# Row sums of a finished chunk, one score run later in a two-layer attention and spectral kernel

## The chip, the cores and the metric

The kernel runs on one core of a Trainium2 chip. The time is that of one execution on the device, in microseconds (us): the median of several runs. One further execution was recorded by the hardware profiler; its rows are what the texts below quote. The engines are PE (TensorE: matmuls, with PEld for its weight loads), DVE (VectorE), ACT (ScalarE), POOL (GpSimd) and SP (SyncE, which here issues DMAs). Each engine runs its own instructions in order; semaphores make one wait for another.

## What is computed

The reference is two layers, each a multi-head attention with a residual, and a filter in the frequency domain with a residual. The attention is what matters here:

```python
def _A_ref(x, wqkv, wo):
    B, S, D = x.shape            # 1, 2048, 1024
    H = 32                       # heads of 32
    Dh = D // H
    qkv = (x @ wqkv).reshape(B, S, 3, H, Dh).transpose(2, 0, 3, 1, 4)
    q, k, v = qkv[0], qkv[1], qkv[2]
    scores = jnp.einsum("bhqd,bhkd->bhqk", q, k) * (Dh ** -0.5)
    p = _softmax(scores, axis=-1)
    o = jnp.einsum("bhqk,bhkd->bhqd", p, v)
    return o.transpose(0, 2, 1, 3).reshape(B, S, D) @ wo
...
x = A_x
x = x + _A_ref(_layernorm(x), A_wqkv, A_wo)
x = x + _B_ref(_layernorm(x), B_w_r, B_w_i)      # rfft2, times W, irfft2
x = x + _A_ref(_layernorm(x), A_wqkv, A_wo)
x = x + _B_ref(_layernorm(x), B_w_r, B_w_i)
```

## The kernel before

The 32 heads are worked on in 8 groups of 4 (`g`, 0 to 7). Within a group the 2048 queries are cut into 4 chunks of 512 (`c`), and the 2048 keys into 16 tiles of 128 (`kt`). One (`c`, `kt`) is a unit; a group has 64 units, a layer 512. For a unit three things are done:

- `S` (line 548 in the profile, called a score run below): 12 matmuls give the scores of four heads in two PSUM tiles `s` (each 128 x 1024, two banks); ACT turns each into exponentials `p` (L552). The scores are transposed: keys stand on the partitions, queries along the free axis. The pool of `s` has three tiles, that of `p` eight.
- `PV` (L558): the value matmuls of the unit, four heads side by side in 32 columns each, add into one PSUM bank `o`, which holds the chunk's output until the 16th unit; then ACT copies it out (L562).
- `add` (L571): DVE adds the two tiles `p` of the unit to two accumulators `acc[0]` and `acc[1]` in SBUF, which in the profile stand under the tile name `R`. Unit 0 of a chunk adds nothing; unit 1 starts the accumulators anew from the tiles of units 0 and 1 (L569), so it overwrites what the chunk before left there. There is one pair of accumulators.

When a chunk is finished, `fin` (lines 573 to 585) makes the divisors of the softmax. Four matmuls of `acc` with a matrix of ones (L577) sum over the partitions into one `s` tile (named `z`); eight records in the profile. DVE transposes `z` (L578), takes the reciprocal (L580), keeps a running maximum (L581), spreads it (L583) and multiplies the copied output by it (L584). Later `out` (L590, L591, L593) writes the product out: a cast on ACT, a difference on POOL, a DMA on SP.

Between these steps a generator, called the filler, puts other work on PE: in every odd unit some 8 to 24 matmuls of the projections for coming groups, Q and K (`qk_chunk`, L328) or V (`v_tiles`, L372). A projection's chunk adds up in one PSUM bank `x` (the pool has one buffer); for Q and K, ACT casts it to its high half (L167) and DVE computes the low half (L168), and only after that may PE write the next projection into `x`. A projection also takes weights that are split in the same way (L168 with `wst`; in the first layer followed by a maximum, L257). When Q or K of a group is whole, four small matmuls (L345) and a reduction on DVE (L347) give its norms, by which the exponentials are shifted. Even groups carry Q and K projections (12 chunks of 24 steps), odd groups one Q and then V. Group 6 loads the output projection's weights beside its units, and group 7 carries that projection's first part (L431, L451).

The order of PE and ACT in this stage is the order in which the code is written (`manual_schedule`); the order of DVE, POOL and SP is chosen by the framework's scheduler when the program is built. The written order around a chunk's end is set by the loop over `u` (printed below). `pend` holds units whose value matmuls are still to come: at each even `kt` the two units before are done in one run of eight matmuls. `late` holds the same units for `add`, one at each unit. So, with units 14 and 15 of chunk c left over:

- unit 0 of the next chunk: scores, then the value matmuls of units 14 and 15, `add` of 14
- unit 1: scores, `add` of 15, and `fin` of the finished chunk; then filler
- unit 2: scores, the value matmuls of units 0 and 1
- unit 3: scores, `add` of 1 (L569), filler
- unit 5: `out`

`fin` is called in the loop 31 times per layer, 62 in all; the last chunk of each layer has its own call behind the loop.

Of the kernel before, what the change touches and what calls it, by code (L numbers as in the profile page):

```python
# [266 lines left out]
def attention(nc, tc, layer, ap, xin, yd, wts, wo, cst, dram, flags):  # L267
# [116 lines left out]
    def sums(ph):  # L384
        return 8 if ph[0] == "v" else 4

    def filler():
        run(prep(phases[0]))
        for i, ph in enumerate(phases):
            nxt = prep(phases[i + 1]) if i + 1 < len(phases) else iter(())  # L390
            for n in range(sums(ph)):
                yield from (v_tiles if ph[0] == "v" else qk_chunk)(ph, n)
                for _ in range(1 + (n > 0)):
                    next(nxt, None)
            run(nxt)
# [6 lines left out]
    def load_wo():  # L402
        st = []

        def load(i):
            if i < 16:
                s = sgp.tile([128, 512], F32, name="wst")
                nc.sync.dma_start(s, wo[i // 2 * 128:i // 2 * 128 + 128, i % 2 * 512:i % 2 * 512 + 512])
                st.append(s)
        load(0)  # L410
        load(1)
        for i in range(16):
            load(i + 2)
            d, sl = i // 2, slice(i % 2 * 512, i % 2 * 512 + 512)
            split(nc, wo_t[0][d // 4][:, d % 4, sl], wo_t[1][d // 4][:, d % 4, sl], st[i], SW)
            yield
# [51 lines left out]
    def wo_parts():  # L468
        load_o(0)
        load_o(1)  # L470
        for t in [2, 3, 0, 1] + list(range(4, 12)):
            if t == 8:
                two = wvp.tile([128, 2, 1024], F32, name="wv")
                wo_dst[8], wo_dst[9] = two[:, 0], two[:, 1]
            yield from wo_part(t // 4, t % 4, wo_dst[t])
            if t in (1, 7):
                load_o(t // 4 + 2)
# [64 lines left out]
    def S(g, c, kt):  # L542

        s = [psS.tile([128, 2, 512], F32, name="s") for _ in range(2)]
        for i, (a, b) in enumerate(((0, 0), (0, 1), (1, 0))):
            for h in range(4):
                r = slice(32 * h, 32 * h + 32)
                nc.tensor.matmul(s[h // 2][:, h % 2], K[g][r, a, kt * 128:kt * 128 + 128],  # L548
                                 Q[g][r, b, c * 512:c * 512 + 512], start=i == 0, stop=i == 2)
        for hf in range(2):  # L550
            p = P[g, c, kt, hf] = pp.tile([128, 2, 512], F32, name="p")
            nc.scalar.activation(p, s[hf], AF.Exp, bias=bias[g], scale=SCALE / (SQ * SQ))  # L552
# [12 lines left out]
    def add(g, c, kt):  # L565
        for hf in range(2):
            p = P[g, c, kt, hf]
            if kt == 1:
                nc.vector.scalar_tensor_tensor(acc[hf], P[g, c, 0, hf], 1e-34, p, op0=ALU.add, op1=ALU.add)  # L569
            elif kt:  # L570
                nc.vector.tensor_add(acc[hf], acc[hf], p)  # L571

    def fin(g, c):
        zt = on.tile([128, 16, 32], F32, name="zt")
        z = psS.tile([128, 2, 512], F32, name="s")[:, 0]
        for h in range(4):
            nc.tensor.matmul(z[32 * h:32 * h + 32], cst["ones"], acc[h // 2][:, h % 2], start=True, stop=True)  # L577
        nc.vector.transpose(zt.rearrange("p a b -> p (a b)"), z)  # L578
        rc = sm.tile([128, 16], F32, name="rc")
        nc.vector.reciprocal(rc, zt[:, :, 0])  # L580
        nc.vector.tensor_max(flags["r"], flags["r"], rc)  # L581
        r = on.tile([128, 512], F32, name="zt")
        nc.vector.transpose(r.rearrange("p (a b) -> p a b", b=32), rc.unsqueeze(2).broadcast_to([128, 16, 32]))  # L583
        nc.vector.scalar_tensor_tensor(r, O[g, c], SO, r, op0=ALU.mult, op1=ALU.mult)  # L584
        O[g, c] = r
# [8 lines left out]
        else:  # L594
            olast[c] = t

    pend, done, late = [], [], []
    fill, lwo, wof = filler(), load_wo(), wo_parts()
    left, parts, rests = 16, 20, list(range(12))

    def slots(f, sums, n, steps):

        while sums:
            k = max(1, int(n / sums + 0.5))
            m = -(-steps // k)
            for i in range(0, steps, m):
                while left_norms:
                    norms()
                for _ in range(min(m, steps - i)):
                    next(f, None)  # L610
                n -= 1
                yield sums - (i + m >= steps)
            sums -= 1

    with tc.manual_schedule(engines={mybir.EngineType.PE, mybir.EngineType.Activation}):
        for g in range(NG):
            todo = sum(sums(ph) for ph in beside.get(g, []))
            sl = slots(fill, todo, 22 if g == NG - 2 else 32, 24)
            wsl = slots(wof, 4, 10, 21)
            for u in range(NCH * NKT):  # L620
                c, kt = divmod(u, NKT)
                S(g, c, kt)
                if kt % 2 == 0:
                    for w in pend:
                        PV(*w)
                    late = pend
                    pend = []
                for w in late[:1]:
                    add(*w)
                    if w[2] == NKT - 1:  # L630
                        fin(*w[:2])
                        done = [w[:2]]
                late = late[1:]
                if kt == 5 and done:
                    out(*done.pop())
                pend.append((g, c, kt))
                if kt % 2 == 0:
                    continue
                if todo:
                    todo = next(sl)  # L640
                elif g == NG - 2:
                    if left:
                        run(lwo)
                        left = 0
                    if next(wsl, None) is not None and u == NCH * NKT - 1:
                        run(wsl)
                elif g == NG - 1:
                    t = rests[0] if rests else 16
                    if (t // 4 < c - 1 or t // 4 == c - 1 and kt >= 7) and (kt % 4 == 3 or not parts):
                        wo_rest(rests.pop(0))  # L650
                    elif parts:
                        parts -= 1
                        for _ in range(21):
                            next(wof)
                if g == NG - 2 and todo < 4:
                    for _ in range(2):
                        if left > (8 if todo == 3 else 0):
                            next(lwo, None)
                            left -= 1
        for w in pend:  # L660
            PV(*w)
        for w in late + pend:
            add(*w)
        run(wof)
        for t in rests:
            wo_rest(t)
# [537 lines left out]
```

## Time and profile before

| what | value |
|---|---|
| median of 3 runs | 3942.41 us (3938.75 to 3947.32) |
| profiled execution | 3932.85 us |
| its span, first to last instruction | 3931.1 us |
| mean granted TensorE clock | 0.987 |
| score stage, first layer | about 130 to 1670 us of the span |
| score stage, second layer | about 2100 to 3620 us of the span |
| largest group of DVE | L571, 1792 adds, 2145.1 us busy |
| largest group of ACT | L552, 2048 exponentials, 2170.0 us busy |
| largest groups of PE | L558 984.9 us, L328 688.8 us, L548 432.3 and 432.0 us busy |

How to read the rows. In a timeline a row has the start in us from the span's start, the busy time in us, the engine, line and operation, then the written tile, an arrow and the tiles read, the shape and the number of instructions that were merged into the row; in square brackets stands the idle time of the engine before it and what ended that. In a table of groups the numbers behind the bar are the busy time in us, the mean of one in ns, and the idle time before the group's instructions with what ended it. "R", "Q", "x", "s", "o", "p" are tile names of the program. A busy PE is not PE at its peak: matmuls overlap, and the ends are modelled; the starts are recorded. Rows are merged, so that a short wait inside a run shows as a longer row and not as idleness.

### The profile page before, as it was taken

What the parts mean: (1) busy time and instruction counts of PE and PEld (TensorE: products, weight loads), DVE (VectorE), ACT (ScalarE), POOL (GpSimd) and SP (SyncE); (2) the same over time, 40 slices, a digit from 0 to 9 for tenths busy, and PEclk for the clock granted to TensorE, in tenths of its full rate; (3) what the DMA queues carried; (4) which work ended last, traced back from release to release, by engine and by line L of the source; (5) the groups of instructions that cost most, each with busy time, mean ns of one, the idle gap of its engine ahead of it and who ended that gap; (6) DMA issues with size and microseconds to landing.
All of it is one profiled execution on the core that took longest, in us unless ns stands there. A gap on an engine that the chain in (4) does not pass through costs nothing.

```text
span 3931.1 us, 80082 instructions
## 1 busy us (share of the span) xinstructions
PE 3764.3 (96%) x33204; PEld 1667.9 (42%) x33204; DVE 3188.9 (81%) x3865; ACT 2896.0 (74%) x3561; POOL 644.0 (16%) x589
## 2 busy tenths in 40 slices
PE   7999999999999999989989999999999999999798
PEld 5322432342233233368863334333432432333688
DVE  6689898989898877866666998899898888788454
ACT  4587887788788765558746888888888787665586
POOL 1111011101110200004321220122021212000143
PEclk9999999999999999999999999999999999999999
DMA  3000000000000211143120000000000002111333
GB/s 116 15 12 22 12 12 17 17 12 20 12 23 9 90 49 68 60 159 125 59 87 12 20 18 12 12 17 23 9 18 17 17 12 89 56 70 56 135 110 105
DMA packets 97560, 177.32 MB, mean 45 GB/s; under 512 B 7200, under 2 KB 52896, under 8 KB 96160
## 3 DMA queue, kind: packets, MB, share of 16 engines
q1 hardware_dynamic: 97040, 172.03, 12.7%
q8 instruction: 262, 4.29, 0.4%
q14 instruction: 114, 0.93, 0.1%
q10 hardware_dynamic: 144, 0.07, 0.0%
HBM read 123.83 MB, written 48.23 MB: 44 GB/s over the span
## 4 chain that ended last, share of the span: by engine, by line


## 5 line engine op out<-in xcount | busy, mean ns | idle before, releaser
L552 ACT ACTIVATE p<-s,bias 128x1024 f32<-128x1024 f32 x2048 | 2170.0, 1112 | 586.2 <-PE s L548 575.1
L571 DVE TENSOR_TENSOR R<-R,p 128x1024 f32<-128x1024 f32 x1792 | 2145.1, 1249 | 145.5 <-ACT p L552 141.3
L558 PE MATMUL o<-p,R 128*32 128x512 f32 x8192 | 984.9, 598 | 0.0
L328 PE MATMUL x<-big,wqk 128*128 128x512 f16 x2880 | 688.8, 385 | 22.9 <-DVE R L168 8.2
L548 PEld LDWEIGHTS <-R 32*128 32x128 f16 x12288 | 231.1, 92 | 782.6 <-issue 666.3
L328 PEld LDWEIGHTS <-wqk 128*128 128x128 f16 x3072 | 278.0, 98 | 463.8 <-issue 173.5
L548 PE MATMUL s<-R 32*128 32x512 f16 x6144 | 432.3, 379 | 19.9 <-ACT p L552 16.4
L548 PE MATMUL s<-Q,R 32*128 32x512 f16 x6144 | 432.0, 378 | 11.9 <-ACT p L552 10.6
L558 PEld LDWEIGHTS o<-p,R 128*32 128x32 f32 x8192 | 213.7, 109 | 523.5 <-issue 523.0
L591 POOL TENSOR_TENSOR ohl<-zt,ohl 128x512 f16<-128x512 f32 x62 | 180.1, 2905 | 1471.9 <-ACT ohl L590 1471.9
L372 PEld LDWEIGHTS <-big 128*128 128x128 f16 x3072 | 292.2, 98 | 116.5 <-issue 69.6
L372 PE MATMUL x<-wv,big 128*128 128x256 f16 x2688 | 321.2, 276 | 12.4 <-DVE R L168 5.8
L569 DVE SCALAR_TENSOR_TENSOR R<-p 128x1024 f32<-128x1024 f32 x128 | 153.8, 1203 | 199.0 <-ACT p L552 198.7
L332 POOL TENSOR_TENSOR sq<-R 128x512 bf16<-128x512 f16 x96 | 142.3, 1482 | 700.3 <-ACT R L167 699.8
L431 PE MATMUL x<-big 128*128 128x512 f16 x1008 | 228.0, 380 | 0.0
L431 PEld LDWEIGHTS <-big 128*128 128x128 f16 x1344 | 126.7, 98 | 177.7 <-issue 35.5
L881 DVE TENSOR_TENSOR H<-G,H 128x512 f16<-128x512 f32 (+1 forms) x68 | 46.7, 687 | 104.5 <-ACT H L880 104.4
L833 PE MATMUL ps<-cbi,H 128*128 128x256 f16 (+1 forms) x792 | 99.1, 273 | 5.6 <-ACT H L880 3.7
L826 ACT COPY U<-ps 64x256 f32<-64x256 f32 (+1 forms) x272 | 97.2, 357 | 8.4 <-PE ps L833 3.3
L826 ACT COPY B<-ps 64x256 f32<-64x256 f32 (+1 forms) x272 | 97.1, 357 | 6.7 <-PE ps L833 2.4
L332 POOL TENSOR_TENSOR sq<-Q 128x512 bf16<-128x512 f16 x32 | 45.1, 1409 | 324.3 <-ACT Q L167 324.3
L833 PE MATMUL ps<-cb,big 128*128 128x256 f16 x780 | 96.3, 273 | 0.0
(419 smaller groups left out, 3100.8 us busy)
## 6 DMA issues: line engine op xcount, KB each, us to landing
wst<-in_wp SPq DMA_DIRECT2D x96, 256.0 KB, 3.0
R<-y SPq DMA_DIRECT2D x32, 512.0 KB, 5.2
w<-in_w SPq DMA_DIRECT2D x60, 256.0 KB, 2.6
od<-ohl SPq DMA_DIRECT2D x56, 256.0 KB, 2.4
big<-od SPq DMA_DIRECT2D x16, 896.0 KB, 7.1
y<-R SPq DMA_DIRECT2D x20, 512.0 KB, 2.6
R<-in_x SPq DMA_DIRECT2D x16, 512.0 KB, 6.7
wst<-in_wo SPq DMA_DIRECT2D x32, 256.0 KB, 2.9
```

What stands on the lines that cost most here:

```text
L328: nc.tensor.matmul(ps, a, b, start=d == 0 and i == 0, stop=d == 7 and i == 2)
L332: nc.gpsimd.tensor_tensor(nrm[ph][:, c], t[:, 0], t[:, 0], op=ALU.mult)
L372: nc.tensor.matmul(ps[:, j], l, r, start=d == 0 and i == 0, stop=d == 7 and i == 2)
L431: nc.tensor.matmul(p, a, b, start=start and d == ds[0] and i == 0, stop=stop and d == ds[-1] and i == 2)
L548: nc.tensor.matmul(s[h // 2][:, h % 2], K[g][r, a, kt * 128:kt * 128 + 128], Q[g][r, b, c * 512:c * 512 + 512], start=i == 0, stop=i == 2)
L552: nc.scalar.activation(p, s[hf], AF.Exp, bias=bias[g], scale=SCALE / (SQ * SQ))
L558: nc.tensor.matmul(O[g, c][32 * h:32 * h + 32], V[g][:, kt, 32 * h:32 * h + 32], P[g, c, kt, h // 2][:, h % 2], start=kt == 0, stop=kt == ...
L569: nc.vector.scalar_tensor_tensor(acc[hf], P[g, c, 0, hf], 1e-34, p, op0=ALU.add, op1=ALU.add)
L571: nc.vector.tensor_add(acc[hf], acc[hf], p)
L591: eng.tensor_tensor(t[:, 1], r, t[:, 0], op=ALU.subtract)
L826: nc.scalar.copy(ov[64 * r:64 * r + 64, a0:a0 + m, x], tl[64 * x:64 * x + 64, :m, r])
L833: nc.tensor.matmul(out, l, r, start=k == 0, stop=k == len(mm_) - 1)
```

## The change

`fin` of the finished chunk is no longer called in unit 1, behind the `add` of unit 15, but in unit 2, behind that unit's scores and ahead of the value matmuls of units 0 and 1. That is the third score run of the new chunk. In unit 1 the chunk is only noted in `ends`. What `fin` does, the number of instructions and the call for the last chunk of a layer, behind the loop, stay as they were.

```diff
-    pend, done, late = [], [], []
+    pend, ends, done, late = [], [], [], []
...
                 S(g, c, kt)
                 if kt % 2 == 0:
+                    if ends and kt == 2:
+                        fin(*ends[0])
+                        done = [ends.pop()]
                     for w in pend:
                         PV(*w)
                     late = pend
...
                 for w in late[:1]:
                     add(*w)
                     if w[2] == NKT - 1:
-                        fin(*w[:2])
-                        done = [w[:2]]
+                        ends = [w[:2]]
                 late = late[1:]
                 if kt == 5 and done:
                     out(*done.pop())
```

## The prediction

> **What bounds the kernel now.** I read the page's busy shares first, then the windows over the score stages, then the groups of PE and DVE, and last the timeline of single engines around the ends of chunks. The page, and one window over most of the first layer's score stage (columns: length, then busy of PE, weight loads, DVE, ACT, POOL, clock, DMA):
>
> ```profile
> PE 3764.3 (96%) x33204; PEld 1667.9 (42%) x33204; DVE 3188.9 (81%) x3865; ACT 2896.0 (74%) x3561; POOL 644.0 (16%) x589
> 170.00:1280.00 1110.00, 1087.91 (x10280) 384.35 (x10276) 1000.50 (x1013) 897.16 (x954) 133.44 (x96) 1.00 0.05 16
> ```
>
> PE sets the pace, 98% busy in this window; but DVE is at 90%, so 2.4 us of new DVE idleness in a chunk of some 45 us takes half of its reserve. The groups (busy, mean ns | idle before, releaser):
>
> ```profile
> L577 PE MATMUL s<-R,ones 128*32 128x512 f32 x512 | 73.1, 604 | 1.4 <-DVE R L571 1.4
> L571 DVE TENSOR_TENSOR R<-R,p 128x1024 f32<-128x1024 f32 x1792 | 2145.1, 1249 | 145.5 <-ACT p L552 141.3
> L569 DVE SCALAR_TENSOR_TENSOR R<-p 128x1024 f32<-128x1024 f32 x128 | 153.8, 1203 | 199.0 <-ACT p L552 198.7 <-PE s L577 0.3
> ```
>
> L577 are the row sums (64 times 8 records). L569 is the first add of the next chunk: it overwrites the accumulator that L577 reads, so it may not run before it; today its 199 us of idleness are ended by exponentials. PE at two chunk ends, then DVE at the first:
>
> ```profile
> 177.28 2.08 PE L577 MATMUL s<-R,ones 128*32 128x512 f32 x8
> 179.29 1.90 PE L328 MATMUL x<-big,wqk 128*128 128x512 f16 x8
> 181.13 0.82 PE L548 MATMUL s<-R 32*128 32x512 f16 x12
> 181.88 1.92 PE L558 MATMUL o<-p,R 128*32 128x512 f32 x16
> ...
> 222.52 1.06 PE L577 MATMUL s<-R,ones 128*32 128x512 f32 x8
> 223.52 2.76 PE L328 MATMUL x<-big,wqk 128*128 128x512 f16 x12
> ```
> ```profile
> 175.90 2.35 DVE L571 TENSOR_TENSOR R<-R,p 128x1024 f32<-128x1024 f32 x2
> 178.54 1.23 DVE L569 SCALAR_TENSOR_TENSOR R<-p 128x1024 f32<-128x1024 f32 x1 [0.28 <-ACT p L552]
> ```
>
> At 177.28 the last adds end at 178.25 and PE loses 1 us (2.08 against 1.06). That is the exception: 73.1 less 64 x 1.065 leaves 4.9 us for all row sums.
>
> **The change, part by part.** On PE, first chunk end of the first layer (s is a score or row-sum tile, o the value product, x the filler's), before and then now:
>
> ```order
> L548 MATMUL s<-R 128x512
> L577 MATMUL s<-R,ones 32x512 x4
> L328 LDWEIGHTS wqk
> L328 MATMUL x<-big,wqk 128x512
> ```
> ```order
> L548 MATMUL s<-R 128x512
> L577 MATMUL s<-R,ones 32x512 x4
> L558 MATMUL o<-p,R 32x512 x8
> L548 LDWEIGHTS R
> ```
>
> The row sums move behind a filler run and a score run. DVE at the same place, before and now:
>
> ```order
> L569 SCALAR_TENSOR_TENSOR R<-p 128x1024
> L578 STREAM_TRANSPOSE zt<-s 128x512
> L569 SCALAR_TENSOR_TENSOR R<-p 128x1024
> L580 RECIPROCAL rc<-zt 128x16
> L168 SCALAR_TENSOR_TENSOR R<-x,R 128x512
> L581 TENSOR_TENSOR fr<-fr,rc 128x16
> L583 STREAM_TRANSPOSE zt<-rc 128x512
> L584 SCALAR_TENSOR_TENSOR zt<-oc,zt 128x512
> L571 TENSOR_TENSOR R<-R,p 128x1024 x12
> ```
> ```order
> L168 SCALAR_TENSOR_TENSOR R<-x,R 128x512
> L569 SCALAR_TENSOR_TENSOR R<-p 128x1024
> L578 STREAM_TRANSPOSE zt<-s 128x512
> L569 SCALAR_TENSOR_TENSOR R<-p 128x1024
> L580 RECIPROCAL rc<-zt 128x16
> L571 TENSOR_TENSOR R<-R,p 128x1024
> L581 TENSOR_TENSOR fr<-fr,rc 128x16
> L583 STREAM_TRANSPOSE zt<-rc 128x512
> L571 TENSOR_TENSOR R<-R,p 128x1024
> L584 SCALAR_TENSOR_TENSOR zt<-oc,zt 128x512
> L571 TENSOR_TENSOR R<-R,p 128x1024 x10
> ```
>
> The filler's split L168 goes ahead where it falls there, two adds slip between the small steps; nothing else jumps the queue. ACT, POOL and SP keep their order, so no DMA moves in its queue.
>
> *What stays covered.* The row sums need a score tile, the one that the second exponential of the score run before frees:
>
> ```profile
> 177.39 2.12 ACT L552 ACTIVATE p<-s,bias 128x1024 f32<-128x1024 f32 x2
> ```
>
> It ends at 179.51, which is 2.23 after the old place of the row sums at 177.28, and the new place comes 2.59 after it: no new wait, by 0.36. ACT's cast L590 needs L584's result; it stands behind the exponentials of the fourth score run after the moved row sums, some 10.9 us after they start (value, score, filler, score, value, score run, exponentials), and L584 is done about 8 us after. Were that cover gone, ACT would stand still in order, and PE with it.
>
> *Gains.* The 4.9 us go: the adds end at most 1 us after the old place, and the new one is 2.6 us later. Beside them, the row sums stand directly ahead of the value matmuls. 8 records take 1.00 (222.52 to 223.52; each run's busy time overlaps the next by 0.06) and 16 take 1.92 - 0.06 = 1.86, so a run costs 2 x 1.00 - 1.86 = 0.14 that doesn't depend on its length, and two runs made one save up to 0.14 at each of 62 places, 8.9 us. If a joined run keeps its 0.14, the sum below is 3.5 higher. The Trainium skill (TensorEngine Tiling (Array Packing), Tiling Modes) says that changing the tiling mode drains the array and changing only the tile doesn't; both runs are 128*32, so by it the whole 0.14 goes; no row of before has such a pair.
>
> *The cost.* L569 waits for the moved row sums, and all DVE work queues behind it. A chunk end of the second layer, PE and then DVE:
>
> ```profile
> 2143.44 1.07 PE L577 MATMUL s<-R,ones 128*32 128x512 f32 x8
> ...
> 2166.01 1.89 PE L328 MATMUL x<-big,wqk 128*128 128x512 f16 x8 [0.36 <-DVE R L168]
> ```
> ```profile
> 2144.69 1.23 DVE L569 SCALAR_TENSOR_TENSOR R<-p 128x1024 f32<-128x1024 f32 x1 [2.12 <-ACT p L552]
> 2145.83 0.71 DVE L578 STREAM_TRANSPOSE zt<-s 128x512 f32<-128x512 f32 x1
> 2146.47 1.18 DVE L569 SCALAR_TENSOR_TENSOR R<-p 128x1024 f32<-128x1024 f32 x1
> 2147.57 0.24 DVE L580 RECIPROCAL rc<-zt 128x16 f32<-128x16 f32 x1
> ...
> 2148.51 0.70 DVE L583 STREAM_TRANSPOSE zt<-rc 128x512 f32<-128x512 f32 x1
> 2149.24 0.69 DVE L584 SCALAR_TENSOR_TENSOR zt<-oc,zt 128x512 f32<-128x512 f32 x1
> 2149.84 15.51 DVE L571 TENSOR_TENSOR R<-R,p 128x1024 f32<-128x1024 f32 x12
> 2165.28 0.68 DVE L168 SCALAR_TENSOR_TENSOR R<-x,R 128x512 f16<-128x512 f32 x1
> ```
> ```profile
> 2161.30 4.06 DVE L571 TENSOR_TENSOR R<-R,p 128x1024 f32<-128x1024 f32 x2
> ```
>
> From the start f of the old row sums: the new ones start at f + 1.84 (filler, 179.29 to 181.13) + 0.75 (scores, to 181.88) = f + 2.59; they end 1.07 later, so L569 starts near f + 3.7 instead of f + 1.25. By start-to-start times, L569 1.14, L578 0.64, L569 1.10, L580 and L581 0.4, L583 0.73, L584 0.60 and two adds at 1.14 make 6.9: DVE stands at f + 10.6 where it stood, after its two adds, at 2149.84 + 2.28 - 2143.44 = f + 8.7. It is 1.9 late. Twelve adds run in one piece (the excess over 1.14 each is mostly slow adds, the row at 2161.30, which is two adds at 2.0, and not waiting), then comes the split L168 that frees the only PSUM bank x, for which PE already waits. So 1.8 reaches PE. Elsewhere the slack between L168's end and PE's next filler is subtracted:
>
> ```profile
> 228.82 2.35 DVE L571 TENSOR_TENSOR R<-R,p 128x1024 f32<-128x1024 f32 x2
> 237.74 1.34 DVE L257 TENSOR_REDUCE wm<-wst 128x1 f32<-128x512 f32 x2 [0.82 <-DMA wst<-in_wp]
> 246.92 0.68 DVE L168 SCALAR_TENSOR_TENSOR Q<-x,Q 128x512 f16<-128x512 f32 x1
> ```
> ```profile
> 247.65 2.53 PE L328 MATMUL x<-big,wqk 128*128 128x512 f16 x11 [2.38 <-DVE Q L168]
> ```
> ```profile
> 502.16 1.06 PE L577 MATMUL s<-R,ones 128*32 128x512 f32 x8
> 518.77 0.60 PE L328 MATMUL x<-big,wqk 128*128 128x512 f16 x2
> ```
> ```profile
> 508.01 9.22 DVE L571 TENSOR_TENSOR R<-R,p 128x1024 f32<-128x1024 f32 x8
> 517.15 0.69 DVE L168 SCALAR_TENSOR_TENSOR R<-x,R 128x512 f16<-128x512 f32 x1
> ```
> ```profile
> 387.12 3.51 PE L372 MATMUL x<-wv,big 128*128 128x256 f16 x16 [2.06 <-DVE R L168]
> ```
> ```profile
> 2293.66 2.36 DVE L571 TENSOR_TENSOR R<-R,p 128x1024 f32<-128x1024 f32 x2 [0.17 <-ACT p L552]
> 2295.94 0.68 DVE L168 SCALAR_TENSOR_TENSOR R<-x,R 128x512 f16<-128x512 f32 x1
> ```
> ```profile
> 2281.61 0.40 PE L345 MATMUL s<-sq,bones 128*32 128x512 bf16 x4 [0.21 <-ACT p L552]
> ...
> 2297.56 1.68 PE L328 MATMUL x<-big,wqk 128*128 128x512 f16 x7
> ```
>
> By kind of chunk end (even and odd g, from chunk to chunk), both layers:
> - even, 0 to 1, 8 places: 1.8; in three of the first layer some 0.5 less, since the old stall goes: 13.
> - even, 1 to 2, 6 places: the filler run at 223.52 is 2.70 long, so the row sums start at f + 3.46, DVE stands at f + 11.5 instead of 228.82 + 2.28 - 222.52 = f + 8.6, 2.9 late. In the first layer the wait for a weight load (0.82 at 237.74) is filled by an add that the new order puts behind the weight splits; the slack at 247.65 is nil, since PE waited there already: 2.0. The second layer has no such wait and no stall: 2.9 less a slack that I take, as below, at 0.9: 12 in all.
> - odd 3 to even 0, 6 places: first add at f + 5.85, so 10.6 - 5.85 - 2.28 = 2.5 late; slack 518.77 - 517.84 = 0.93: 1.5 each: 9.
> - even 3 to odd 0, 6 places: the same slack, 2297.56 - 2296.62 = 0.94 (the last rows), 0.17 of DVE's waiting that takes up lateness, and the 0.2 that the norm matmuls (L345) wait there for a score tile behind the row sums goes: 1.2: 7.
> - odd 0 to 1: PE waits for L168 at 387.12 in the first layer, 3 places. The chunk begins 1.2 late by the kind before, so that only part of a new 1.8 is added: between 0 and 1.8, taken at 1.3: 4. In the second layer no PE wait on L168 stands there, and I count none.
> - even 2 to 3 (6) and g = 6, 1 to 2 (2): between 0 and 1.9, taken at 0.9: 7.
> - the other 25, with V products or output projection beside them: no split that PE waits for, -0.14 each: -3.5.
>
> The sum is +48 us. The profiled execution took 3932.85 (span 3931.1), so 3981 by it; the runs' median is 3942.41, 9.6 higher, so 3990. The measurement can tell some 0.2% (8 us) from no change.
>
> **Rivals.** *The lateness is swallowed.* Then only gains are left: 4.9, 1.3 (six times the 0.21 at 2281.61) and 8.9: -15, 3927. For it: DVE has 110 us idle in that window. Against it: no idleness stands between the row sums and L168 at 2165.28 or 517.15. It decides from the point at which DVE idles 1.9 ahead of that split. 0.07.
>
> *Only places where PE already waits pay.* The eight, three and three places above with a wait in their rows give 13 + 6 + 4 = 23, less the 15: +8, 3950, within 0.2%. It needs the slack elsewhere to be 1.5 more than the rows show. 0.07.
>
> *The longer waits cost clock too.* One wait of 2.1 us was followed by twelve slow filler matmuls:
>
> ```profile
> 614.45 4.07 PE L328 MATMUL x<-big,wqk 128*128 128x512 f16 x12 [2.08 <-DVE Q L168]
> ```
>
> against 2.76 at 223.52, 1.3 more; at 247.65 no such loss followed 2.38. Six waits of the first layer, the three like 247.65 and the three like 387.12, grow to about 4: 6 x 1.3 to 2.6 is 8 to 16, so 3998 to 4006. The Trainium skill (TensorE: Matmul & The Clock Gate, Part 1) puts half clock behind an idle window of about 3.4 us, which speaks for this case. 0.2.
>
> *The change doesn't do what it says*: the order of PE above rules it out.
>
> **How the numbers follow.** The main case has 0.66, with 3972 to 4000 as its own range: lower if L569 may start half a microsecond earlier (some 32 places, -16), higher with the unknown kinds at 1.9. The range 3957 to 4008 adds the clock case and part of the rest. Slower: 0.66 + 0.2 = 0.86; same 0.07; faster 0.07.
>
> **What would show it.** Right: L569's idleness grows from 199 to about 330 us and its releaser becomes L577; L577 falls to some 66 busy; the idleness of PE ahead of its filler (below for L328), which L168 ends, grows by some 45 in all; row sums and value matmuls together take 2.72, not 2.86.
>
> ```profile
> L328 PE MATMUL x<-big,wqk 128*128 128x512 f16 x2880 | 688.8, 385 | 22.9 <-DVE R L168 8.2 <-DVE Q L168 6.5 <-ACT wqk L167 5.4
> ```
>
> Wrong: L328's idleness stays near 23 us, or L569 still starts 1.25 after the score run ahead of the row sums' old place.

## The result, and the profile after

| | before | after |
|---|---|---|
| median of 4 runs | 3940.58 us (3935.93 to 3947.32) | 4050.73 us (4044.13 to 4057.25) |
| profiled execution's span | 3931.1 us | 4052.0 us |
| mean granted clock | 0.987 | 0.975 |
| ratio after / before | | 1.0282, 95% interval 1.027 to 1.0295 |

The change costs 110 us. The forecast said slower, by the mechanism that came, but by 48 us; 4050.7 lies outside its range of 3957 to 4008.

The page of after, and then the groups that the prediction named (busy, mean ns of one | idle before, releaser):

```profile
PE 3796.4 (94%) x33204; PEld 1688.2 (42%) x33204; DVE 3203.0 (79%) x3865; ACT 2893.7 (71%) x3561; POOL 577.9 (14%) x589
```
```profile
L571 DVE TENSOR_TENSOR R<-R,p 128x1024 f32<-128x1024 f32 x1792 | 2182.5, 1268 | 116.9 <-ACT p L552 115.1
L328 PE MATMUL x<-big,wqk 128*128 128x512 f16 x2880 | 716.2, 396 | 107.8 <-DVE R L168 70.6 <-DVE Q L168 28.8 <-ACT wqk L167 5.4
L569 DVE SCALAR_TENSOR_TENSOR R<-p 128x1024 f32<-128x1024 f32 x128 | 155.6, 1217 | 183.3 <-PE s L577 139.7 <-ACT p L552 43.5
L577 PE MATMUL s<-R,ones 128*32 128x512 f32 x512 | 68.2, 605 | 0.0
```

The row sums (L577) lost their stalls, 73.1 to 68.2. L569's main releaser is now L577, 139.7 us. And L328's idle time went from 22.9 to 107.8 us, where 45 more were forecast. Its busy time went from 688.8 to 716.2 as well: the same 2880 records of filler matmuls take 27 us longer. The span's 121 us are 32 more of PE's busy time (3764.3 to 3796.4) and 89 of its idle time.

The waits of PE on the low-half split, the view of waits of before and then of after (us in total, times, longest):

```profile
PE x L328 <- DVE R L168: 8.2, 8, 2.4
...
PE x L328 <- DVE Q L168: 6.5, 3, 2.4
PE x L372 <- DVE R L168: 5.8, 3, 2.1
```
```profile
PE x L328 <- DVE R L168: 70.6, 29, 3.1
PE x L328 <- DVE Q L168: 28.8, 8, 5.0
...
PE x L372 <- DVE R L168: 23.9, 6, 4.7
```

20.5 us became 123.3, in 43 waits in place of 14. So the chain of the prediction is there: row sums later, L569 later, DVE late, split late, PE waits for its bank.

One place shows why the waits are twice as long as forecast. It is the end from an odd group to an even one whose rows of before stand in the prediction (502.16 to 518.77). PE of after, from the moved row sums on:

```profile
521.66 1.06 PE L577 MATMUL s<-R,ones 128*32 128x512 f32 x8
522.54 1.90 PE L558 MATMUL o<-p,R 128*32 128x512 f32 x16
...
534.78 0.83 PE L548 MATMUL s<-R 32*128 32x512 f16 x12
538.71 2.72 PE L328 MATMUL x<-big,wqk 128*128 128x512 f16 x6 [3.10 <-DVE R L168]
```

DVE of after at the same place, then POOL of after, and POOL of before at its place:

```profile
522.81 1.23 DVE L569 SCALAR_TENSOR_TENSOR R<-p 128x1024 f32<-128x1024 f32 x1 [6.23 <-PE s L577]
...
529.34 8.71 DVE L571 TENSOR_TENSOR R<-R,p 128x1024 f32<-128x1024 f32 x6
535.99 2.06 DVE L571 TENSOR_TENSOR R<-R,p 128x1024 f32<-128x1024 f32 x1
537.97 0.68 DVE L168 SCALAR_TENSOR_TENSOR R<-x,R 128x512 f16<-128x512 f32 x1
```
```profile
533.14 1.85 POOL L591 TENSOR_TENSOR ohl<-zt,ohl 128x512 f16<-128x512 f32 x1 [43.14 <-ACT ohl L590]
534.95 2.02 POOL L332 TENSOR_TENSOR sq<-R 128x512 bf16<-128x512 f16 x1
```
```profile
516.43 1.82 POOL L591 TENSOR_TENSOR ohl<-zt,ohl 128x512 f16<-128x512 f32 x1 [43.54 <-ACT ohl L590]
518.22 2.02 POOL L332 TENSOR_TENSOR sq<-R 128x512 bf16<-128x512 f16 x1
```

The six adds from 529.34 to L168 take 537.97 - 529.34 = 8.63 us; at 1.14 each they would take 6.84. The row at 535.99, from a narrower window, shows the last of these six alone; it takes 2.06: it is the one that meets POOL's square L332, and the one ahead of it meets the difference L591. In before, L591 began at 516.43 and L168 at 517.15: no add stood between the two, and those that POOL slowed came behind the split. DVE's lateness has carried the way to the split into POOL's work. The add at 535.99 ends at 538.05, 1.08 after L332's end at 536.97, which is about an add's usual 1.14: it stood still until POOL was done. The Trainium skill (SBUF — State Buffer, "SBUF: two separate sides") says that a VectorE step with two inputs in SBUF, as an add is, and a GpSimd step share one pair of ports as an exclusive lock, held for a whole instruction, and that the other side blocks; this trace agrees, with the 1.08 us.

Counted over the 40 chunk ends with a split of the filler behind them, in one trace of each kernel: of the adds between L569 and the first such split, 80 took over 1.5 us in after (two at every end) and 19 in before, and all these adds together took 52.5 us longer. The split began 3.05 us later in the mean, measured from the chunk's first score run; 1.3 of that are the slow adds, the other 1.7 are the lateness that L569's wait leaves.

What follows the wait, in windows of after (columns as in the prediction's first window: length, PE, weight loads, DVE, ACT, POOL, clock, DMA):

```profile
534.43:537.84 3.41, 1.18 (x16) 0.32 (x13) 3.41 (x2) 3.26 (x4) 2.54 (x2) 1.00 0.23 77
537.84:541.26 3.42, 2.55 (x7) 0.88 (x7) 3.42 (x5) 0.00 (x0) 0.00 (x0) 0.50 0.02 5
541.26:544.67 3.41, 3.41 (x23) 0.80 (x25) 1.93 (x2) 0.96 (x1) 0.00 (x0) 0.50 0.00 0
```

The granted clock is 0.50 from 537.84, still within the wait, to 544.67. The row at 538.71 shows six of the filler run's eight matmuls, as its view ends there: they take 2.72, where all eight took 1.90 at 179.29 in before.

The starts of the score runs in the two traces give the loss of each chunk (start of its first score run to that of the next chunk's, after minus before). By the prediction's kinds, with two controls that are told below beside it (all in us, each from one profiled execution of each kernel):

| chunk end | places | forecast | measured | run e2 (late DVE, no move on PE) | POOL's steps mostly left out (e13 less e14) |
|---|---|---|---|---|---|
| even, 0 to 1 | 8 | 13 | 17.4 | 17.7 | 6.3 |
| even, 1 to 2 | 6 | 12 | 26.4 | 17.3 | 15.2 |
| odd 3 to even 0 | 6 | 9 | 28.0 | 22.7 | 7.2 |
| even 3 to odd 0 | 6 | 7 | 26.1 | 23.4 | 5.5 |
| odd 0 to 1, first layer | 3 | 4 | 6.7 | 10.8 | 3.5 |
| even 2 to 3, and g = 6, 1 to 2 | 8 | 7 | 5.3 | 16.6 | 1.9 |
| other | 25 | -3.5 | 8.0 | 9.6 | 6.7 |
| sum | 62 | 48 | 117.9 | 118.1 | 46.3 |

Nearly all of the change's loss sits in the units whose filler waits for the split, 7, 9 or 13 of a chunk, and in the unit behind. At chunk ends where PE waits for no later step of DVE it is -0.14 each: the unit without the row sums is 1.00 shorter, the one with them 0.86 longer.

### The profile page after: what moved, and what is told of

Its sections match the earlier page's. It is cut to its first block, busy times and chain, and to the rows that moved or that the text cites. A ratio compares the mean times of both kernels' runs of the same rounds, so it can differ in the third digit from the quotient of the medians.

```text
span 4052.0 us, 79970 instructions
## 1 busy us (share of the span) xinstructions
PE 3796.4 (94%) x33204; PEld 1688.2 (42%) x33204; DVE 3203.0 (79%) x3865; ACT 2893.7 (71%) x3561; POOL 577.9 (14%) x589
## 4 chain that ended last, share of the span: by engine, by line
## 5 line engine op out<-in xcount | busy, mean ns | idle before, releaser
L571 DVE TENSOR_TENSOR R<-R,p 128x1024 f32<-128x1024 f32 x1792 | 2182.5, 1268 | 116.9 <-ACT p L552 115.1
L328 PE MATMUL x<-big,wqk 128*128 128x512 f16 x2880 | 716.2, 396 | 107.8 <-DVE R L168 70.6
L328 PEld LDWEIGHTS <-wqk 128*128 128x128 f16 x3072 | 285.4, 100 | 549.0 <-issue 270.7
L548 PE MATMUL s<-Q,R 32*128 32x512 f16 x6144 | 434.4, 379 | 15.2 <-ACT p L552 10.6
L372 PE MATMUL x<-wv,big 128*128 128x256 f16 x2688 | 325.9, 278 | 29.9 <-DVE R L168 23.9
L591 POOL TENSOR_TENSOR ohl<-zt,ohl 128x512 f16<-128x512 f32 x62 | 111.2, 1793 | 1504.8 <-ACT ohl L590 1504.8
L569 DVE SCALAR_TENSOR_TENSOR R<-p 128x1024 f32<-128x1024 f32 x128 | 155.6, 1217 | 183.3 <-PE s L577 139.7
L332 POOL TENSOR_TENSOR sq<-R 128x512 bf16<-128x512 f16 x96 | 148.0, 1542 | 773.2 <-ACT R L167 772.7
L168 DVE SCALAR_TENSOR_TENSOR R<-x,R 128x512 f16<-128x512 f32 x88 | 60.1, 683 | 78.9 <-ACT R L167 78.9
L332 POOL TENSOR_TENSOR sq<-Q 128x512 bf16<-128x512 f16 x32 | 43.8, 1370 | 386.5 <-ACT Q L167 386.5
```

The lines of the kernel that those rows point to most:

```text
L328: nc.tensor.matmul(ps, a, b, start=d == 0 and i == 0, stop=d == 7 and i == 2)
L332: nc.gpsimd.tensor_tensor(nrm[ph][:, c], t[:, 0], t[:, 0], op=ALU.mult)
L372: nc.tensor.matmul(ps[:, j], l, r, start=d == 0 and i == 0, stop=d == 7 and i == 2)
L591: eng.tensor_tensor(t[:, 1], r, t[:, 0], op=ALU.subtract)
```

## The experiments

The main theory: L569 waits for the moved row sums, DVE is late, POOL's steps then meet the adds ahead of the split, PE waits for the split and is slowed by half clock behind it. The rivals: PE's own new order costs the time; the excess is clock alone; the forecast's terms were too small by themselves. Each run stands beside runs of the kernel before on the same chip; "the third run" in an expectation is e3, and so on.

### e1. Without the wait: row sums of another tile

```diff
-            nc.tensor.matmul(z[...], cst["ones"], acc[h // 2][:, h % 2], start=True, stop=True)
+            nc.tensor.matmul(z[...], cst["ones"], P[g, c, NKT - 1, h // 2][:, h % 2], start=True, stop=True)
...
-        nc.vector.reciprocal(rc, zt[:, :, 0])
+        nc.vector.tensor_scalar(rc, zt[:, :, 0], 0.0, 1.0, op0=ALU.mult, op1=ALU.add)
```

> The changed kernel, but the moved row sums read the exponentials of the chunk's last unit in place of the accumulators (the sums are of one unit only, and the reciprocal is replaced by a constant of one, so no softmax comes out; the number of instructions stays). Nothing that overwrites an accumulator waits for the row sums any more. If the loss is DVE's wait at L569 (main theory), it goes whole and only the gains are left: about 3925 to 3935 us, L569's idle time back near 200 us with exponentials as its releaser, PE's idle time ahead of L328 near 20 us. If the loss is in PE's own new order (rival: the row sums between score run and value matmuls hold a score tile too long, or cost clock), PE's order is the same as in the changed kernel and the time stays near 4050.

Measured: 3934.98 us, ratio to before 0.9989 (0.998 to 0.9999). Two groups of this run:

```profile
L328 PE MATMUL x<-big,wqk 128*128 128x512 f16 x2880 | 692.6, 386 | 29.9 <-DVE R L168 14.1 <-DVE Q L168 8.2 <-ACT wqk L167 5.4
L569 DVE SCALAR_TENSOR_TENSOR R<-p 128x1024 f32<-128x1024 f32 x128 | 152.1, 1229 | 178.0 <-ACT p L552 177.8
```

PE issues the same matmuls in the same order as in the changed kernel, and the whole loss is gone; L569 is released by exponentials again. The rival of PE's own order falls. The gains forecast with no wait were 15 us; 4 to 5 came, because some waits and half clock were added (the table under "The clock" has them). L328 idles 29.9, against 22.9 in before: at the ends 0 to 1 and 2 to 3 of even groups, where this trace is 3.2 and 3.3 us slower than that of before, a few splits are still a little later.

### e2 and e8. Late without waiting: three more small transposes, then one

```diff
-        nc.vector.transpose(r.rearrange(...), rc.unsqueeze(2).broadcast_to([128, 16, 32]))
+        [nc.vector.transpose(r.rearrange(...), rc.unsqueeze(2).broadcast_to([128, 16, 32])) for _ in range(4)]
```

> The kernel before, with the second small transpose (L583) done four times in place of once: 3 x 0.73 = 2.2 us of DVE work at each chunk end, about as much as the changed kernel's DVE stands idle there, and no move on PE. If lateness of DVE as such is the cause, with POOL's work then colliding and PE waiting for L168, the time rises by 80 to 120 us, to 4020 to 4060, with PE waiting in the same units (the 8th and the 10th of a chunk). If the cause is the waiting for PE or PE's order, 2.2 us of DVE work are taken from the 110 us of idleness that DVE has, and it stays within 20 us: 3940 to 3960.

Measured: 4054.07 us, ratio 1.0283 (1.0266 to 1.03). The second run has `range(2)` in place of `range(4)`.

> The kernel before with the small transpose twice in place of four times: 0.73 us of lateness in place of 2.2. If the loss is in proportion, 114/3 = 38 us: 3975 to 3985. If the slack of about 0.9 us that the forecast counted at most chunk ends is real, only the places where PE waits already pay, some 17 of 0.7 us: 3945 to 3962.

Measured: 3956.76 us, ratio 1.0043 (1.0026 to 1.0059). The filler's group in the run with three more and then in the run with one more:

```profile
L328 PE MATMUL x<-big,wqk 128*128 128x512 f16 x2880 | 711.3, 394 | 94.2 <-DVE R L168 65.7 <-DVE Q L168 20.1 <-ACT wqk L167 5.4
```
```profile
L328 PE MATMUL x<-big,wqk 128*128 128x512 f16 x2880 | 688.8, 385 | 29.9 <-DVE R L168 13.0 <-DVE Q L168 8.1 <-ACT wqk L167 5.4
```

2.2 us of DVE work at each chunk end cost 114 us, as much as the change, with nothing moved on PE, and by the table above mostly at the same ends (more of it from 2 to 3, less from 1 to 2). It is lateness as such that costs. But 0.73 us cost only 18: not in proportion. The slack that the forecast counted is real; the table's three kinds with a counted slack (1 to 2, odd 3 to even 0, even 3 to odd 0) lose nothing in that run's trace (0.1 us or less).

### e7. Half the way

`fin` is called ahead of the third score run, behind the filler of the second unit.

```diff
-                S(g, c, kt)
-                if kt % 2 == 0:
-                    if ends and kt == 2:
-                        fin(*ends[0])
-                        done = [ends.pop()]
+                if ends and kt == 2:
+                    fin(*ends[0])
+                    done = [ends.pop()]
+                S(g, c, kt)
+                if kt % 2 == 0:
```

> The row sums half as far: still ahead of the third score run, behind the filler run of the second unit, so 0.75 us earlier than in the changed kernel. If the loss follows DVE's lateness step by step, some 45 chunk ends get 0.75 us back, and part of the half-clock stretches, while the 0.14 of the joined runs is lost again: 3995 to 4020. If the loss comes at one blow, as soon as DVE is late enough to meet POOL ahead of the split, it stays above 4030 or falls below 3970.

Measured: 3992.95 us, ratio 1.0138 (1.0121 to 1.0155), 2 us below the range named.

```profile
L328 PE MATMUL x<-big,wqk 128*128 128x512 f16 x2880 | 695.3, 387 | 60.8 <-DVE R L168 38.0 <-DVE Q L168 15.0 <-ACT wqk L167 5.4
```

The loss is 54 us: 0.75 us earlier takes 56 of the 110 away, more than 45 chunk ends times 0.75 = 34. So the last three quarters of a microsecond are the dear ones. Together with the two runs above (0.73 us: 18; 2.2 us: 114) the cost grows faster than the lateness, but no single blow shows.

### e3 and e4. POOL's difference out of the way

```diff
-                if kt == 5 and done:
+                if kt == (5 if g == NG - 1 else 11) and done:
                     out(*done.pop())
```

> The changed kernel, with the writing out of a finished chunk (cast on ACT, difference on POOL, DMA) six units later, behind the splits that PE waits for; in the last group as it was. DVE's order stays the same row by row. If part of the loss is POOL's difference (L591) slowing adds ahead of the split (2.2 us in place of 1.2 in the trace), about 1 us goes at some 20 places, and clock with it: 25 to 45 us less, 4005 to 4025. If POOL plays no part and the excess over the forecast is clock or plain lateness, it stays within 10 us of 4050.

> The kernel before with the same later writing out, as the control for the run above. There the trace shows the slow adds mostly behind the split, so little is to be had: 3930 to 3942 by either theory. If it falls by as much as the changed kernel does (25 us or more), the later writing out is a gain of its own and tells nothing of the change.

Measured: 3999.41 us, ratio 1.0149 (1.0132 to 1.0166), for the changed kernel, and 3918.84, ratio 0.9944 (0.9927 to 0.996), for the kernel before. Both predictions were too small: 51 and 21 us fell. The loss of the change went from 110 to 81 us, so 30 us of it hung on where POOL's difference falls; and the later writing out is a gain of its own. The same end of chunk in the second layer, the changed kernel and then this run:

```profile
2563.48 1.89 PE L328 MATMUL x<-big,wqk 128*128 128x512 f16 x8 [3.09 <-DVE R L168]
2565.30 0.83 PE L548 MATMUL s<-R 32*128 32x512 f16 x12
```
```profile
2530.34 3.15 PE L328 MATMUL x<-big,wqk 128*128 128x512 f16 x8 [2.12 <-DVE R L168]
2533.43 1.19 PE L548 MATMUL s<-R 32*128 32x512 f16 x12
```

The wait is 1 us shorter, as expected of one slow add less. But here the shorter wait was followed by half clock (3.15 in place of 1.89 for the same eight matmuls) and the longer one was not; this place gained nothing. The last section shows what tells the two apart.

### e5, e6, e13 and e14. POOL's steps mostly left out

```diff
-        nc.gpsimd.tensor_tensor(nrm[ph][:, c], t[:, 0], t[:, 0], op=ALU.mult)
+        c or nc.gpsimd.tensor_tensor(nrm[ph][:, c], t[:, 0], t[:, 0], op=ALU.mult)
...
-        eng.tensor_tensor(t[:, 1], r, t[:, 0], op=ALU.subtract)
+        g < NG - 1 or eng.tensor_tensor(t[:, 1], r, t[:, 0], op=ALU.subtract)
...
```

In the lines left out here the norms are taken from the one square that is kept, and the high half of the output is stored twice.

> The changed kernel with most of POOL's work in the score stage left out: the difference L591 of all groups but the last (the high half is stored twice in its place), and three of the four squares L332 of each projection (the norms come from one chunk's squares). The run before this one took the difference alone out of the way, and 51 us went, of which the kernel before has 21 as well; the split's wait at the end from an odd group to an even one then still held one slow add beside L332. If both of POOL's steps lengthen the way to the split (main theory), the loss against the quiet kernel before falls from 110 us to 45 to 65, near the forecast of 48, and PE's wait at that place falls from 3.1 to about 1.2 us: 3950 to 3985. If POOL's part was the difference alone, the loss stays at 80.

> The kernel before with the same work of POOL left out, as the control: no more than the later writing out brought, plus a little: 3900 to 3925 by either theory.

Measured: 3959.01 us, ratio 1.0048 (1.0032 to 1.0065), and 3891.36, ratio 0.9879 (0.9863 to 0.9896). The loss is 68 us: it fell, a little less than expected. At the place shown above (odd to even group) PE still waits 2.12, where 1.2 was expected; the square of the projection's first chunk, the one kept, falls just there. The next two runs keep the third chunk's square in its place (`c != 2 or` for `c or`).

> As the fifth run, but the one square per projection that stays is that of its third chunk and no longer of its first. In the fifth run's trace the first chunk's square still slowed one add ahead of the split at the two ends between groups (PE's wait 2.12 us there, where 1.2 was expected). If those squares are what is left of the excess over the forecast, some 12 places get 0.9 us back and part of the half clock: the loss against its control falls from 68 to between 45 and 58 us. If the forecast's own terms were too small, it stays above 62.

> The control: the kernel before with the same work left out. By either theory within 8 us of the sixth run, 3884 to 3900.

Measured: 3950.35 us, ratio 1.0038 (1.0023 to 1.0052), and 3900.87, ratio 0.9913 (0.9896 to 0.9929). The loss is 49.5 us. The same place in the fifth run and then in this one:

```profile
521.49 0.81 PE L328 MATMUL x<-big,wqk 128*128 128x512 f16 x3 [2.12 <-DVE R L168]
```
```profile
520.52 1.89 PE L328 MATMUL x<-big,wqk 128*128 128x512 f16 x8 [1.28 <-DVE R L168]
```

1.28 us without POOL's steps, where the forecast had 1.5 for this kind, joined runs included. The groups of the changed kernel in this form, and then of its control:

```profile
L571 DVE TENSOR_TENSOR R<-R,p 128x1024 f32<-128x1024 f32 x1792 | 2095.1, 1219 | 95.5 <-ACT p L552 92.6
L328 PE MATMUL x<-big,wqk 128*128 128x512 f16 x2880 | 689.2, 385 | 49.9 <-DVE R L168 23.5 <-DVE Q L168 18.0 <-ACT wqk L167 5.4
```
```profile
L571 DVE TENSOR_TENSOR R<-R,p 128x1024 f32<-128x1024 f32 x1792 | 2105.8, 1224 | 164.2 <-ACT p L552 159.2
L328 PE MATMUL x<-big,wqk 128*128 128x512 f16 x2880 | 685.5, 383 | 19.2 <-DVE Q L168 5.9 <-DVE R L168 5.8 <-ACT wqk L167 5.4
```

With POOL mostly still, L328's idle time grows by 31 us in place of 85 and its busy time by 3.7 in place of 27.4. One reservation: of the fall from 68 to 49.5 about half (9 us) is the changed kernel's and half is the control's rise, which missed its range by 1 us: the third chunk's square seems to cost the kernel before something that the first chunk's doesn't.

### e15, e11 and e12. The same with all work kept

Later writing out, and the squares on DVE (`nc.vector` for `nc.gpsimd` in L332) or on ACT (`activation` with `AF.Square`).

> The changed kernel with all of its work kept, the writing out later and the squares on DVE, beside 3906 for the kernel before in that form. POOL meets no add ahead of a split; but each projection's square is 0.47 us more on DVE, behind the split. If POOL's part is as the quiet runs say, the loss is 55 to 75 us: 3960 to 3980. If the quiet runs owed their small loss to the work left out, it is near 110 again: 4010 or more.

> A candidate that keeps all of the work: the kernel before with the writing out six units later, and the squares L332 computed on DVE in place of POOL, so that nothing of POOL meets the adds ahead of a split. It takes away some 66 slow adds of 0.9 us and adds 128 steps of DVE whose price no trace shows, between 0.3 and 0.7 us each: 3890 to 3930, against 3919 with the later writing out alone.

> The same with the squares on ACT, right behind the cast of the high half: 128 steps of some 0.6 us between exponentials, on an engine that is 74% busy. If ACT has the room, 3880 to 3915; if the later exponentials hold up PE, 3930 or more.

Measured: the changed kernel 3965.35 us, ratio 1.0078 (1.0061 to 1.0095). The kernel before with the squares on DVE 3906.10, ratio 0.9919 (0.9902 to 0.9935); on ACT 3910.69, ratio 0.9926 (0.9909 to 0.9943). One square on DVE and on ACT:

```profile
L332 DVE TENSOR_TENSOR sq<-R 128x512 bf16<-128x512 f16 x96 | 44.7, 466 | 0.0
```
```profile
L332 ACT ACTIVATE sq<-R 128x512 bf16<-128x512 f16 x96 | 60.5, 630 | 3.0
```

The loss is 59 us by the medians, 63 by the ratios, within the 55 to 75 expected: it isn't the left-out work that made it smaller. The two versions without the change are faster than both kernels, by 0.7 to 0.8% against before and 3.5 to 3.6% against after; their own difference can't be told.

### e9 and e10. The split ahead of the adds: a test that went too far

DVE's order in the stage as written, and outside the chunk ends the adds of two units written behind the filler of the second; the writing out is six units later, as in e3:

```diff
-    with tc.manual_schedule(engines={mybir.EngineType.PE, mybir.EngineType.Activation}):
+    with tc.manual_schedule(engines={mybir.EngineType.PE, mybir.EngineType.Activation, mybir.EngineType.DVE}):
...
+                while owe and kt % 2 == 0:
+                    add(*owe.pop(0))
                 S(g, c, kt)
...
+                if kt > 1:
+                    owe, late = owe + late, []
                 for w in late[:1]:
                     add(*w)
...
```

> The changed kernel with DVE's order in the score stage as it is written, and the adds written so that the low-half split L168 stands ahead of up to four adds more than now; the writing out six units later as in the third run. L569 waits for the moved row sums as before, so DVE is as late as in the changed kernel, but PE no longer waits for that lateness. If the loss is lateness that reaches PE through the split (main theory), most of it goes: 3900 to 3945, against 3999 with the later writing out alone. If DVE's lost time itself is what counts, PE waits elsewhere (for exponentials, whose buffers the adds free) and the time stays above 3970.

> The control for the run above: the kernel before with the same order on DVE and the same later writing out. Main theory: the change costs little once the split stands first, so within 25 us of the run above, 3895 to 3935. If DVE's lost time counts, 60 us or more below the run above.

Measured: 4373.63 us, ratio 1.1096 (1.1076 to 1.1116), and 4569.91, ratio 1.1595 (1.1576 to 1.1615). Both far off. Waits of DVE and of PE in the first of them, a group of it, and a wait of PE in the control:

```profile
DVE R L168 <- ACT R L167: 349.7, 71, 11.5
```
```profile
PE s L548 <- ACT p L552: 281.6, 208, 4.2
```
```profile
L328 PE MATMUL x<-big,wqk 128*128 128x512 f16 x2880 | 731.8, 402 | 7.6 <-ACT wqk L167 5.4 <-ACT big L167 1.9
```
```profile
PE s L577 <- DVE R L571: 164.0, 45, 4.9
```

PE no longer waits for the split (7.6 us idle, none of it for L168). But DVE, in order, now stands 350 us at a split whose cast ACT has not made, the adds behind it free the exponentials' buffers late, and PE waits 282 us ahead of scores. The control also waits 164 us for its adds at the old place of the row sums, so the two can't be compared, and the question that the pair was made for (what the change costs when the split is out of the way) stays open. A milder order, the split ahead of one or two adds, was not tried.

## Why the prediction was right and wrong

**What bounds the kernel, and the mechanism: right.** L569 waits for the moved row sums; without that wait the loss is gone (3935 us), and lateness of DVE without any move on PE costs the same (4054). It reaches PE through the split, as forecast: 103 us more of PE's waits are on L168.

**DVE's idle time.** L569's own idle time did not grow (199.0 to 183.3), though L577 became its releaser. A part of the wait stands in other rows: the scheduler put splits ahead of L569, and these now do the waiting. The groups of L168 in before and in after:

```profile
L168 DVE SCALAR_TENSOR_TENSOR R<-x,R 128x512 f16<-128x512 f32 x88 | 59.1, 672 | 16.4 <-ACT R L167 16.4
```
```profile
L168 DVE SCALAR_TENSOR_TENSOR R<-x,R 128x512 f16<-128x512 f32 x88 | 60.1, 683 | 78.9 <-ACT R L167 78.9
```

Idle time in front of one line is no measure of lateness where the order moves with it.

**The failed step: what DVE does between the chunk's end and the split.** The prediction priced each add at 1.14 us, saw that the excess over it "is mostly slow adds, the row at 2161.30", and took these as the same before and after. They were not: 2 us of lateness brought the adds ahead of the split into the time of L591 and L332, two slow adds at each of the 40 ends where there had been 19 in all. L571's busy time rose by 37 us (2145.1 to 2182.5); with POOL mostly still it is 2095 and 2106 in the two kernels. The waits that were forecast to grow by 45 us grew by 103. (The 45 was short of the prediction's own sum, whose six priced kinds make 52; the 52.5 us more that the adds ahead of the splits took are about the rest.) With POOL's steps left out the loss is 49.5 us against the 48 of the sum, and its kinds are near the forecast's where they were furthest off: 7.2 and 5.5 against 9 and 7 at the ends between groups, measured 28.0 and 26.1 with POOL. So the sum was about right for a kernel in which little else runs beside DVE, but that the total comes so near is in part luck, as errors cancel: the ends 0 to 1 came out at 6 against 13, 1 to 2 at 15 against 12, and the 25 others at +7 against -3.5, because the second layer's odd groups and the last group also wait for a late step of DVE, which the prediction counted as none.

**The clock.** The main case priced half clock at nothing; the rival "the longer waits cost clock too" had a chance of 0.2 and 8 to 16 us, at six waits. It was right in kind and far too small. The traces' records of the granted clock give the size. In the score stages (from the first score run of each layer to its last) the length of two kernels differs by PE's idle time, by half of the time in which PE was busy at a clock of 0.50 (an estimate: at 0.50 the fillers at 538.71 are spaced 0.43 us apart, in before 0.22), and by a rest, which holds the gains:

| us, one trace of each | length | PE idle | half clock | rest |
|---|---|---|---|---|
| after less before | 117.3 | 89.4 | 45.0 | -17.0 |
| e13 less e14 | 45.7 | 47.4 | 7.7 | -9.4 |
| e2 less before | 118.2 | 86.4 | 32.9 | -1.1 |
| e1 less before | 3.3 | 9.3 | 9.2 | -15.2 |

The rest is near nothing in e2, where nothing moved on PE, and the 15 us of the forecast's gains in e1, which has them and little else. So of the 72 us between the loss with POOL's steps and the loss without, 42 are idle time and 37 half clock, less 8 of gains. The half clock goes back to the step above: the waits became more (43 for 14) and longer, and long ones cost clock.

**Gains.** Right: the stalls of L577 are gone (73.1 to 68.2), and the row sums start 0.88 ahead of the value matmuls in place of 1.00 ahead of a filler (522.54 - 521.66); in all 0.14 per place, as the chunk ends with no split behind them show. The Trainium skill (TensorEngine Tiling (Array Packing), Tiling Modes) says that changing the tiling mode, and not just the tile, drains the array; both runs are 128*32, and the trace agrees, with 0.14 saved where they adjoin.

**Cover.** ACT's cast L590 was not held up: at the place shown POOL's L591, which follows it, starts 11.48 us after the moved row sums (533.14 - 521.66), 14.27 after the old ones in before (516.43 - 502.16); the move itself is 2.59 of the difference, so the cast kept its turn on ACT.

**Other rivals.** "The lateness is swallowed" and "only places where PE already waits pay" fell: 29 waits of L328 on the split in place of 8.

## What to carry to other kernels

Before an operation is made later on an in-order engine, list what other engines do in the time into which its followers will fall, not only what stands beside them now: a step that shares a path with the late engine can double the lateness. Price a late engine by its next hand-over to the engine that bounds the kernel; where that engine's clock falls after a wait, the price of a wait is more than its length, and a wait made a little longer can cost much more. And the cheapest test of such a chain is to delay the suspected engine on purpose, with nothing else moved.

## What the runs showed of the hardware

**Half clock comes in slices of 3.41 us, and PE's idle time within one slice decides.** In the clock records of all 17 traces a stretch at 0.50 lasts 3.41 us or a multiple of it (except where the trace ends within it), and in each trace these stretches begin on one fixed grid of 3.41 us. Cut by this grid, the score stages of the 15 traces in the usual order (all but the two with DVE's order by hand) give, for slices at full clock:

| PE idle in the slice, us | slices | the next one at half clock |
|---|---|---|
| under 1.5 | 12932 | 0 |
| 1.5 to 1.7 | 48 | 3 |
| 1.7 to 2.0 | 58 | 21 |
| 2.0 to 2.1 | 19 | 17 |
| over 2.1 | 146 | 146 |

A slice at half clock was followed by another in all 57 cases in which PE idled over 0.8 us in it, as from 537.84 above. So a wait costs clock by where it lies. The prediction priced the clock by two waits of before, one without and one with loss (247.65, 2.38 us of waiting; 614.45, 2.08 us). Their slices, as windows:

```profile
243.67:247.08 3.41, 1.60 (x20) 0.32 (x13) 3.41 (x4) 2.92 (x4) 1.11 (x1) 1.00 0.00 0
247.08:250.49 3.41, 2.84 (x16) 1.19 (x19) 3.41 (x4) 0.34 (x1) 0.00 (x0) 1.00 0.00 0
```
```profile
612.31:615.72 3.41, 1.33 (x10) 0.66 (x7) 3.41 (x5) 2.12 (x2) 0.00 (x0) 1.00 0.00 0
615.72:619.13 3.41, 3.41 (x15) 1.03 (x17) 3.21 (x3) 0.00 (x0) 0.00 (x0) 0.50 0.00 0
```

The longer wait falls into two slices (3.41 - 1.60 = 1.81 us idle, then 0.57) and costs no clock; the shorter one lies in a single slice (2.08) and does. So it is with the two waits of e3's place: 3.09 us in after are 1.56 and 1.53, while the 2.12 of e3 lie in one slice. The grid lies differently in each trace (one of its points is at 18.39 us of the span in before, at 19.02 in after), so a price has to go by odds: half clock followed 5 of 112 waits of 1 to 2 us ahead of fillers, 32 of 59 of 2 to 2.5, and all 19 over 4. The Trainium skill (TensorE: Matmul & The Clock Gate, Part 1) puts half clock behind an idle window of about 3.4 us and says that the window runs freely. The grid agrees with a free-running window of that length; that 2.1 us of idle time within it were always enough here does not fit a window that must be idle throughout.

**POOL and DVE block each other, and either may lose.** POOL's difference L591 in before and in after:

```profile
L591 POOL TENSOR_TENSOR ohl<-zt,ohl 128x512 f16<-128x512 f32 x62 | 180.1, 2905 | 1471.9 <-ACT ohl L590 1471.9
```
```profile
L591 POOL TENSOR_TENSOR ohl<-zt,ohl 128x512 f16<-128x512 f32 x62 | 111.2, 1793 | 1504.8 <-ACT ohl L590 1504.8
```

In before 16 of the 62 steps took 4.5 to 9.3 us: POOL stood still through several adds, which ran at 1.22. In after no step took over 2.3, and the adds stood still. That POOL's mean step got faster was a sign of the loss, not of a gain. What decides which side blocks at a given meeting was not tried.
